# A one-core attention and feed-forward kernel: the 32x32 transposes of w3 read side-by-side columns and write to PSUM, the first block of w3 is turned by products with the identity, and the instructions stand in a new order

## The chip, the core and the metric

The kernel runs on one core of one Trainium2 chip. The metric is the device time of one execution in microseconds (us), lower is better. A profile is one execution, recorded instruction by instruction; its span reaches from the first to the last instruction of the program.

The engines are named as in the profile: PE is TensorE's matmul, PEld its weight load, DVE is VectorE, ACT is ScalarE, POOL is GpSimd, SP is SyncE, which here only issues DMAs. SBUF is the on-chip memory, PSUM the memory that TensorE writes its products to: eight banks, of 512 float32 columns each as the kernel uses them.

## What is computed

The reference is a Nystrom attention over 8 batches, 8 heads, 576 positions and 64 features per head, followed by a feed-forward part on the 4608 rows of width 512:

```python
def _attn_ref(q, k, v):
    q_lm = q.reshape(B, H, 32, S // 32, D).mean(axis=3)
    k_lm = k.reshape(B, H, 32, S // 32, D).mean(axis=3)
    A, Bm, C = sm(q, k_lm), sm(q_lm, k_lm), sm(q_lm, k)
    Z = Bm.transpose(0, 1, 3, 2) / (norm1(Bm) * norminf(Bm) + 1e-06)
    for _ in range(6):
        Z = 2 * Z - Z @ Bm @ Z
    return A @ Z @ C @ v

def _moe_ref(x, w1, w2, w3, w_out):
    a, b = x @ w1, x @ w2        # 512 -> 1024
    return (a * b @ w3) @ w_out  # 1024 -> 1024 -> 512
```

`sm` is a softmax of the scaled products. All inputs and the output are float32.

## The kernel before

**Two stages that overlap.** The kernel multiplies w3 by w_out once, into a float16 matrix `w34` of 1024 x 512, so that the dense part is `(a * b) @ w34`. Row block j (128 rows, j = 0 to 7) of `w34` needs row block j of w3, turned so that w3's columns lie on the partitions, and all of w_out. The first stage of the execution makes `w34`, block after block, and beside it the attention of the first batches. The dense part of batch 0 begins when all eight blocks and the first attention are done; from there on the dense part of one batch runs beside the attention of later ones, to the end.

**One block of w3.** For block j the steps are: `w3n{j}`, SP loads the 128 x 1024 float32 block (`load_w3`, line 323; for j = 0 in one DMA, for the others in four DMAs of 32 partitions, which put the quarter a of the columns on partitions 32a to 32a+31). `wt{j}{h}` turns it. For j = 0 TensorE does it with eight 128x128 transposes (`w3_ptr`, line 355) into three PSUM banks, in pieces of 1, 3 and 4. For j = 1 to 7 VectorE does it in two halves h (`w3_tr`, line 366): it transposes every 32x32 square, which together with the split over partitions by the DMA gives the turned block. The columns of one square are 8 apart in SBUF (`"p (b x c) -> p c b x"`, c = 8), and the result goes to the SBUF tiles `w3f`. `wh{j}{h}` on ACT (line 375) scales the result by 16 and rounds it to float16 (the high part), `wl{j}{h}` on DVE (line 382) makes the float16 remainder (the low part). TensorE then sums, over eight chunks c, high x high, high x low and low x high (`mh`, `mm`; 24 matmuls of 128 x 128 x 512 per block), and `wo{j}` on ACT (line 400) evicts the block. w_out is cut into high and low parts in the same way, chunk by chunk (`wf{c}` the load, `woh{c}` on ACT, `wol{c}` on DVE at line 341; for the chunks listed in `PWL` ACT scales at line 347 and POOL subtracts at line 352).

**One pair of heads-groups.** Task number n (0 to 15) is four heads of a batch. POOL issues the loads of k and q (`lq`, line 464, which also round to float16), SP those of v (`lv`, lines 475 and 478). DVE transposes in 32x32 squares (line 494, reading side-by-side columns); the mean over 18 positions is made by TensorE for n < 4 and by POOL after that (lines 502 and 509); then scores, softmax (DVE and ACT), and the normalisation `an` on POOL (line 654), which waits for DVE's reciprocal of line 648. POOL also issues the eight loads `lw` of w1 and w2 (line 484), which the first product of the dense part's up-projection (`U000`) needs, as it needs `wT` of the first group from DVE (line 893).

**What sets the order.** Each step is a task with an engine, an assumed duration, dependencies and a priority. A list scheduler in the kernel (`Plan.run`) places them with these assumed durations, and the instructions of each engine are then written out in the order found. On the chip each engine runs its own list in order and waits by semaphores; the assumed durations are no longer seen. So a change of an assumed duration or of a priority constant changes only the order. Rings of buffers (`P.ring`) are part of it: PSUM's six banks are the ring `P`.

Of the kernel before, what the change touches and what calls it, by code (L numbers as in the profile page):

```python
# [8 lines left out]
FP32 = mybir.dt.float32  # L9
# [6 lines left out]
S = 576  # L16
# [5 lines left out]
DM = 512  # L22
DF = 1024
HALF = 288
MP = 1.8
MT = 11.0
MY = 4.0
GR = int(2.0)
THIRD = 192
# [15 lines left out]
class Plan:  # L45
# [124 lines left out]
def kernel(  # L170
# [21 lines left out]
    def bank(i):  # L192
        return banks[i]
# [47 lines left out]
    def at(key, i=0):  # L241
        return P.slot[key][i]
# [19 lines left out]
    def att(n):  # L262
        bs = GROUPS[GOF[n // 2][0]]
        k = n - 2 * bs[0] - 2 * len(bs) + 4
        first = dense(bs[0]) - 51.0 + 8.0 * k
        return max(3.0 + 6.0 * n, first)

    def lane(g):
        return dense(GROUPS[g][0]) - 22.0

    def cvt(b):
        g, i = GOF[b]
        return lane(g) - 10.0 + 3.0 * (i + 2 - len(GROUPS[g]))

    NE = int(4.0)
    L0 = 4.0
    UO = 3.0
    GO = 8.0

# [19 lines left out]
    def const_e():  # L299
        nc.gpsimd.memset(vball[64:128, :, :, 4, :], 0.0)  # L300
        nc.gpsimd.memset(ecTall[64:128, :, 4, :], 0.0)
        nc.gpsimd.memset(lmTall, 0.0)

    def pads():
        for T in Tqs:
# [5 lines left out]
    add("cb", "POOL", 0.3, const_b, deps=["ca"], prio=-9)  # L311
    add("cc", "DVE", 0.8, const_c, deps=["cb"], prio=-5.0)
    add("cd", "ACT", 0.16, const_d, deps=["cb"], prio=-4.0)
    add("ce", "POOL", 2.8, const_e, prio=-4.0)


    def load_wout(c):
        def fn():
            nc.sync.dma_start(out=wof[at(f"wf{c}")],
                              in_=moe_w_out.rearrange("(p k) f -> k p f", k=8)[c])  # L320
        return fn

    def load_w3(j):
# [30 lines left out]

    def w3_ptr(j, h, c0, c1):
        def fn():
            ps, src = bank(at(f"ptr{j}{h}")), w3n[at(f"w3n{j}")].rearrange("p (x c) -> p c x", c=8)
            for c in range(c0, c1):
                nc.tensor.transpose(out=ps[:, 128 * (c - c0):128 * (c - c0) + 128], in_=src[:, c],
                                    identity=ident[:, :])  # L360
        return fn

    def w3_src(j, h, c0, c1):
        return bank(at(f"ptr{j}{h}"))[:, 0:128 * (c1 - c0)] if j < PEB else w3f[at(f"w3f{j}")][:, 128 * c0:128 * c1]

    def w3_tr(j, h):
        def fn():
            src = w3n[at(f"w3n{j}")].rearrange("p (b x c) -> p c b x", b=4, x=32)
            out_ = w3f[at(f"w3f{j}")].rearrange("p (c b y) -> p c b y", b=4, y=32)
            nc.vector.transpose(out=out_[:, 4 * h:4 * h + 4], in_=src[:, 4 * h:4 * h + 4])  # L370
        return fn

    def w3_hi(j, h, c0, c1):
# [5 lines left out]
    def w3_lo(j, h, c0, c1):  # L379
        def fn():  # L380
            c, t = slice(128 * c0, 128 * c1), w3t[at(f"w3t{j}")]
            nc.vector.scalar_tensor_tensor(out=t[:, 1, c], in0=w3_src(j, h, c0, c1), scalar=WSC,  # L382
                                           in1=t[:, 0, c], op0=ALU.mult, op1=ALU.subtract)
        return fn
# [16 lines left out]
                                 scale=1.0 / (WSC * WSC))  # L401
        return fn

    W1 = 1.0
    JS = int(4.0)
    JH = 2.0
    PWL = [(), (3,), (1, 4), (1, 3, 5), (1, 3, 5, 7)][int(3.0)]
    PEB = int(1.0)
    FIRST = [(0, 1), (1, 4), (4, 8)] if PEB else [(0, 4), (4, 8)]

    def w34_tasks():
        for j in range(8):
# [17 lines left out]
            for h, (c0, c1) in enumerate(cuts):  # L430
                k = (c1 - c0) / 4
                deps = [f"w3n{j}"] + ([f"wt{j}{h - 1}"] if h else [])
                if j < PEB:
                    add(f"wt{j}{h}", "PE", 0.44 * k, w3_ptr(j, h, c0, c1), deps=deps + ["cb"],
                        acq=[("P", f"ptr{j}{h}", 1, 2)], rel=[f"w3n{j}"], prio=p0 - 4.0 + h, mode="full")
                    src = f"ptr{j}{h}"
                else:
                    add(f"wt{j}{h}", "DVE", 0.62, w3_tr(j, h), deps=deps,
                        acq=[] if h else [("w3f", f"w3f{j}", 1, 4)], rel=[f"w3n{j}"], prio=p0 - 4.0 + 0.1 * h)
                    src = f"w3f{j}"  # L440
                add(f"wh{j}{h}", "ACT", 0.13 + 0.35 * k, w3_hi(j, h, c0, c1), deps=[f"wt{j}{h}"] + ([f"wh{j}0"] if h else []),
                    acq=[] if h else [("w3t", f"w3t{j}", 1, 8)], rel=[src], prio=p0 - 3.5 + h)
                add(f"wl{j}{h}", "DVE", 0.1 + 0.5 * k, w3_lo(j, h, c0, c1), deps=[f"wh{j}{h}"], rel=[src],
                    prio=p0 - 3.5 + h)
            part = {c: h for h, (c0, c1) in enumerate(cuts) for c in range(c0, c1)}
            for c in range(8):
# [233 lines left out]
    def quad_tasks(n):  # L680
# [16 lines left out]
        else:  # L697
# [4 lines left out]
                rel=[f"ls{n}"], prio=p - 5.0)  # L702
        add(f"lt{n}", "DVE", 0.24, lm_trans(n), deps=[f"tk{n}", f"mc{n}"], acq=[("lmu", f"lmu{n}", 1, 1)],
            rel=[f"lm{n}"], prio=p - 2.0)
        add(f"lc{n}", "ACT", 0.8, lm_place(n), deps=[f"lt{n}", "ce"], acq=[("lmT", f"lmT{n}", 1, 3)],
            rel=[f"lmu{n}"], prio=p - 1.5)
        both = [f"lc{n}"]
        add(f"S{n}", "PE", 0.52, s_mm(n), deps=both + [f"tk{n}"],
# [9 lines left out]
        add(f"sm{n}", "DVE", 0.8, s_max(n), deps=[f"S{n}"], acq=[("tiny", f"mx{n}", 1, 1)], prio=p)  # L718
# [377 lines left out]
    P.ring("w3n", 4)  # L1096
    P.ring("wf", 8)
    P.ring("w3t", 2)
    P.ring("w3f", 2)
    for i in range(NCH):  # L1100
        P.ring(f"ab{i}", 1)
    w34_tasks()
    for s in range(2):
        for qd in range(2):
            for wi in range(2):
                add(f"lw{s}{qd}{wi}", "POOL", 0.62, load_w12(s, qd, wi), prio=T0 - 13.0 + qd, after=T0 - 13.0 - 4.0,
                    move=1.46, lat=2.0)
    for n in range(NQ):
        quad_tasks(n)
# [10 lines left out]
    with tc.manual_schedule():  # L1120
        with tc.tile_pool(name="w34pool", bufs=1) as wp:
            w3n = [obig[:, 2 * i:2 * i + 2, :].rearrange("p a x -> p (a x)") for i in range(2)]
            w3n += [wp.tile([128, DF], FP32, name=f"w3n{i}") for i in (2, 3)]
            wof = [ecTs[i][:, 0:4, :].rearrange("p c x -> p (c x)") for i in range(4)]
            wof += [uu[i // 2][:, i % 2, :].bitcast(FP32) for i in range(4)]
            w3t = uu[2:4]
            wo = wp.tile([128, 2, 8, DM], FP16, name="wo")
            w3f = [wp.tile([128, DF], FP32, name=f"w3f{i}") for i in range(2)]
# [36 lines left out]
```

## Time and profile before

| | |
|---|---|
| time, median of 3 runs | 280.5 us (279.28, 280.71, 280.5) |
| the profiled execution: its time | 281.79 us |
| the profiled execution: its span | 280.0 us, granted TensorE clock 0.998 |
| busy share of the span | PE 93%, DVE 69%, ACT 70%, POOL 41% |
| DMA | 37.32 MB, 133 GB/s in the mean |
| the chain of waits, by engine | PE 67%, DMA 15%, ACT 5%, DVE 4% |

The shares are means over a first stage (to about 81 us), in which TensorE has gaps, and a second one in which it has almost none. DMA is in use by 0.8 to 1.1 of its 16 engines' time in the first 80 us and far less after that. The order within the first stage: block 0 of w3 is turned from 4.4 us, the last one (j = 7) from 71.23 us; the eight evictions `wo{j}` stand at 21.5 to 91.9 us; the first up-projection starts at 84.17 us.

### The profile page before, as it was taken

To read this page: it belongs to the slowest core of one execution; us is meant where nothing else is said; L and a number is where in the kernel's file an instruction comes from. 1 tells how busy PE (TensorE), PEld (TensorE's weight loads), DVE (VectorE), ACT (ScalarE), POOL (GpSimd) and SP (SyncE) were. 2 spreads that over 40 slices of the span, in tenths; PEclk is the share of its full clock that TensorE was granted. 3 is DMA by queue.
4 is the path that set the end of the run, shared out by engine and by line. 5 is a ranking of instruction groups with operands and counts; after the bars stand their busy time and mean duration, and the time that the engine had idled before them with its cause. 6 is when DMAs were issued, how large, how long until landed. Compare 5 with 4: busy or idle time off the path is not lost.

```text
span 280.0 us, 9565 instructions
## 1 busy us (share of the span) xinstructions
PE 260.4 (93%) x3824; PEld 169.5 (61%) x3824; DVE 192.3 (69%) x512; ACT 195.1 (70%) x551; POOL 113.8 (41%) x135
## 2 busy tenths in 40 slices
PE   3897679998899999999999999999999999999993
PEld 2244345553554885767677767667875674775762
DVE  3976799999978679776877777757666462442430
ACT  4645544963759988957888896589768656759551
POOL 9540381999499958899736011003001000000000
PEclk9999999999999999999999999999999999999999
DMA  7999899999964743999645431211121102121123
GB/s 226 304 231 251 228 193 241 220 195 217 230 118 86 116 93 49 256 239 208 126 125 159 135 117 40 69 46 41 56 63 40 42 37 77 57 96 40 75 77 114
DMA packets 30620, 37.32 MB, mean 133 GB/s; under 512 B 7792, under 2 KB 19824, under 8 KB 30576
## 3 DMA queue, kind: packets, MB, share of 16 engines
q1 hardware_dynamic: 24576, 24.92, 30.6%
q0 software_dynamic: 5760, 11.54, 23.8%
q8 instruction: 30, 0.49, 0.7%
q10 hardware_dynamic: 240, 0.26, 0.3%
q14 instruction: 14, 0.11, 0.1%
HBM read 38.80 MB, written 9.44 MB: 172 GB/s over the span
## 4 chain that ended last, share of the span: by engine, by line
PE 67%; DMA 15%; ACT 5%; DVE 4%; SPq 3%; issue 2%; POOL 2%; ACTq 0%
PE bank L247 61%; DMA vb<-in_v_dram 6%; DMA w3n<-in_moe_w_dram 5%; PE wide L247 4%; DMA w<-in_moe_w_dram 3%; PE wide L580 2%; DMA ecT<-in_moe_w_out_dram 2%; ACT lmT L539 2%; SPq L475 1%; ACT ec L572 1%; PE bank L663 1%; POOL ls L502 1%; POOL w L484 1%; DVE u L382 1%; SPq L331 1%
## 5 line engine op out<-in xcount | busy, mean ns | idle before, releaser
L247 PEld LDWEIGHTS <-u 128*128 128x128 f16 x960 | 80.3, 98 | 35.6 <-issue 7.4
L1000 DVE TENSOR_TENSOR ab<-asb,bank 128x192 f16<-128x192 f16 x192 | 60.6, 348 | 44.0 <-ACT asb L994 43.7
L247 PE MATMUL bank<-aT,u 128*128 128x192 f16 x768 | 78.6, 246 | 0.2
L247 PE MATMUL bank<-w,ab 128*128 128x512 f16 (+1 forms) x296 | 73.2, 373 | 0.0
L994 ACT CAST asb<-bank 128x192 f16<-128x192 f32 x192 | 56.4, 332 | 23.2 <-PE bank L247 20.4
L247 PE MATMUL bank<-wo,u 128*128 128x512 f16 x192 | 50.7, 394 | 2.0 <-ACT u L375 1.0
L654 POOL TENSOR_TENSOR ah<-ea,tiny 128x512 f16<-128x512 f32 (+1 forms) x16 | 18.7, 1173 | 76.5 <-DVE tiny L648 35.8
L247 PEld LDWEIGHTS <-ab 128*128 128x128 f16 x296 | 27.3, 98 | 20.7 <-issue 2.7
L509 POOL TENSOR_TENSOR ls<-ls 128x128 f32<-128x128 f32 (+2 forms) x48 | 36.1, 752 | 3.5
L911 ACT CAST u<-bank 128x512 f16<-128x512 f32 x64 | 34.3, 602 | 3.5 <-PE bank L247 3.2
L502 POOL TENSOR_TENSOR ls<-nat 128x1152 f32<-128x1152 f16 x12 | 29.0, 2413 | 13.1 <-ACT lm L516 13.0
L1026 ACT ACTIVATE osb<-bank 128x512 f32<-128x512 f32 x35 | 21.1, 603 | 11.6 <-PE bank L247 11.5
L539 ACT COPY lmT<-lmu 32x128 f16<-32x128 f16 x64 | 18.8, 294 | 4.2 <-DVE lmu L530 3.5
L247 PE MATMUL bank<-w,wT 64*32 64x512 f16 x512 | 18.5, 380 | 0.0
L247 PE MATMUL bank<-xz 32*32 32x64 f32 (+1 forms) x768 | 14.8, 213 | 1.4 <-DVE xz L857 1.4
L247 PEld LDWEIGHTS bank<-xz 32*32 32x32 f32 x768 | 11.1, 105 | 7.1 <-DVE xz L857 2.6
L572 ACT ACTIVATE ec<-wide,tiny 128x576 f32<-128x576 f32 x16 | 12.0, 750 | 4.7 <-DVE bsc L566 4.4
L641 ACT ACTIVATE ea<-ea 128x512 f32<-128x512 f32 (+1 forms) x16 | 11.0, 687 | 5.2 <-DVE ea L632 5.0
L375 ACT ACTIVATE u<-w3f 128x512 f16<-128x512 f32 x14 | 8.7, 629 | 8.2 <-DVE w3f L370 8.1
L647 DVE TENSOR_REDUCE tiny<-ea 128x16 f32<-128x512 f32 (+1 forms) x16 | 11.7, 734 | 2.7 <-ACT ea L641 2.7
L247 PEld LDWEIGHTS <-Tq 128*128 128x128 f16 x160 | 10.3, 97 | 5.4 <-issue 3.4
L558 DVE TENSOR_REDUCE tiny<-wide 128x1 f32<-128x576 f32 x16 | 11.7, 732 | 2.2 <-PE wide L247 2.1
(97 smaller groups left out, 330.2 us busy)
## 6 DMA issues: line engine op xcount, KB each, us to landing
vb<-in_v_dram SPq DMA_DIRECT2D x64, 128.0 KB, 4.6
out_dram<-osb SPq DMA_DIRECT2D x37, 128.0 KB, 2.3
nat<-in_k_dram POOLq DMA_DIRECT2D x16, 288.0 KB, 5.4
nat<-in_q_dram POOLq DMA_DIRECT2D x16, 288.0 KB, 7.1
out_dram<-osb SPq DMA_DIRECT2D x16, 256.0 KB, 2.6
w3n<-in_moe_w_dram SPq DMA_DIRECT2D x16, 128.0 KB, 7.4
w<-in_moe_w_dram POOLq DMA_DIRECT2D x8, 256.0 KB, 11.1
osb<-in_moe_w_dram SPq DMA_DIRECT2D x12, 128.0 KB, 4.1
```

What stands on the lines that cost most here:

```text
L247: nc.tensor.matmul(out_, lhsT, rhs, start=start, stop=stop, **({} if pos is None else {"tile_position": pos}))
L502: nc.gpsimd.tensor_tensor(out=l, in0=nat[:, :, 0:9, :], in1=nat[:, :, 9:18, :], op=ALU.add)
L509: nc.gpsimd.tensor_tensor(out=l[:, :, x:x + m, :], in0=l[:, :, x:x + m, :], in1=l[:, :, y:y + m, :], op=ALU.add)
L539: nc.scalar.copy(out=lm[r, :, h, :], in_=u[r].rearrange("p t l e -> p t (l e)"))
L558: nc.vector.reduce_max(out=mx[:, 0:1], in_=s_cols(), axis=AX.X)
L572: nc.scalar.activation(out=ecs[at(f"ec{n}")], in_=s_cols(), func=AXF.Exp, scale=SCALE, bias=tinies[at(f"mx{n}")][:, 1:2], accum_out=tinies ...
L647: nc.vector.reduce_sum(out=t[:, 20:20 + g], in_=eas[at(f"ea{n}")][:, 0:g, :], axis=AX.X)
L654: nc.gpsimd.tensor_tensor(out=ahs[at(f"ah{n}")][:, 0:g, :], in0=eas[at(f"ea{n}")][:, 0:g, :], in1=tinies[at(f"ta{n}")][:, 0:g].unsqueeze(2 ...
L911: nc.scalar.copy(out=uu[at(f"u{b}{qd}")][:, wi, 512 * half:512 * half + 512], in_=bank(at(f"pU{b}{wi}{half}{qd}")))
L994: nc.scalar.copy(out=asb[at(f"as{b}{j}{th}")], in_=bank(at(f"pD{b}{j}{th}"))[:, 0:THIRD])
L1000: nc.vector.tensor_mul(ab[:, j, c0:c0 + THIRD], asb[at(f"as{b}{j}{th}")], bank(at(f"pD{b}{j}{th}"))[:, THIRD:2 * THIRD])
L1026: nc.scalar.activation(out=osb[at(f"os{t}")], in_=bank(at(f"pE{t}")), func=AXF.Copy, scale=2.0 ** -12)
```

## The change

- The split over partitions of w3's columns becomes a = quarter, then c = chunk, then x = one of 32 columns, so that a 32x32 square has its 32 columns side by side. The rows of w_out are loaded in the order that fits it (`load_wout`): chunk c now holds, for each quarter a, 32 rows that lie one after the other.
- `w3_tr` reads those columns and writes to a PSUM bank of the ring `P`, one bank per half, in place of the SBUF tiles `w3f`, which are gone. `wh` and `wl` read the bank.
- `w3_ptr`, for block 0, makes four matmuls of a 128x32 weight with the 128x128 float32 identity in place of each transpose, one for each quarter of the columns, 32 matmuls in all.
- The constants: of w_out's chunks only number 3 is subtracted on POOL (before 1, 3 and 5); ACT's scaling of the other two goes away and DVE makes their low parts. The order's constants MP, MT, W1, JS, JH, L0 and some priorities and assumed durations change. The identity (`cb`) is made before the memsets of `ce`, and the largest of those runs on float32 words, half as many.
- What this does to the lists: SP issues chunks 1 to 4 of w_out ahead of block 1 of w3. POOL issues the eight loads of w1 and w2 after, and no longer before, the four sums of line 509 for n = 6, and two normalisations `an` stand among them: three loads, `an3`, two loads, `an4`, three loads. On TensorE, after the last product of `w34`, the tile shape changes 91 times, before 89 times.

```diff
-MP = 1.8
-MT = 11.0
+MP = 2.4
+MT = 8.0
...
-        return max(3.0 + 6.0 * n, first)
+        return max(6.0 + 6.0 * n, first)
...
-        return lane(g) - 10.0 + 3.0 * (i + 2 - len(GROUPS[g]))
+        return lane(g) - 8.0 + 3.0 * (i + 2 - len(GROUPS[g]))
...
-    L0 = 4.0
+    L0 = 3.0
...
-        nc.gpsimd.memset(lmTall, 0.0)
+        nc.gpsimd.memset(lmTall.rearrange("p i a l e -> p (i a l e)").bitcast(FP32), 0.0)
...
-    add("ce", "POOL", 2.8, const_e, prio=-4.0)
+    add("ce", "POOL", 2.4, const_e, deps=["cb"], prio=-4.0)
...
-                              in_=moe_w_out.rearrange("(p k) f -> k p f", k=8)[c])
+                              in_=moe_w_out.rearrange("(a k x) f -> k a x f", a=4, x=32)[c])
...
-            ps, src = bank(at(f"ptr{j}{h}")), w3n[at(f"w3n{j}")].rearrange("p (x c) -> p c x", c=8)
+            ps, src = bank(at(f"ptr{j}{h}")), w3n[at(f"w3n{j}")]
             for c in range(c0, c1):
-                nc.tensor.transpose(out=ps[:, 128 * (c - c0):128 * (c - c0) + 128], in_=src[:, c],
-                                    identity=ident[:, :])
+                for a in range(4):
+                    mm(ps[32 * a:32 * a + 32, 128 * (c - c0):128 * (c - c0) + 128],
+                       src[:, 256 * a + 32 * c:256 * a + 32 * c + 32], ident[:, :], pos=(0, 32 * a))
...
-        return bank(at(f"ptr{j}{h}"))[:, 0:128 * (c1 - c0)] if j < PEB else w3f[at(f"w3f{j}")][:, 128 * c0:128 * c1]
+        return bank(at(f"ptr{j}{h}"))[:, 0:128 * (c1 - c0)]
...
-            src = w3n[at(f"w3n{j}")].rearrange("p (b x c) -> p c b x", b=4, x=32)
-            out_ = w3f[at(f"w3f{j}")].rearrange("p (c b y) -> p c b y", b=4, y=32)
-            nc.vector.transpose(out=out_[:, 4 * h:4 * h + 4], in_=src[:, 4 * h:4 * h + 4])
+            src = w3n[at(f"w3n{j}")].rearrange("p (b c x) -> p c b x", b=4, x=32)
+            nc.vector.transpose(out=bank(at(f"ptr{j}{h}")).rearrange("p (c b y) -> p c b y", b=4, y=32),
+                                in_=src[:, 4 * h:4 * h + 4])
...
-    W1 = 1.0
-    JS = int(4.0)
-    JH = 2.0
-    PWL = [(), (3,), (1, 4), (1, 3, 5), (1, 3, 5, 7)][int(3.0)]
+    W1 = 5.0
+    JS = int(3.0)
+    JH = 3.0
+    PWL = [(), (3,), (1, 4), (1, 3, 5), (1, 3, 5, 7)][int(1.0)]
...
-                    add(f"wt{j}{h}", "DVE", 0.62, w3_tr(j, h), deps=deps,
-                        acq=[] if h else [("w3f", f"w3f{j}", 1, 4)], rel=[f"w3n{j}"], prio=p0 - 4.0 + 0.1 * h)
+                pe = j < PEB
+                add(f"wt{j}{h}", "PE" if pe else "DVE", 0.86 * k + 0.03 if pe else 0.64,
+                    (w3_ptr if pe else lambda j, h, c0, c1: w3_tr(j, h))(j, h, c0, c1), deps=deps + ["cb"],
+                    acq=[("P", f"ptr{j}{h}", 1, 2)], rel=[f"w3n{j}"], prio=p0 - 4.0 + h, mode="128x32" if pe else None)
...
-        add(f"lc{n}", "ACT", 0.8, lm_place(n), deps=[f"lt{n}", "ce"], acq=[("lmT", f"lmT{n}", 1, 3)],
+        add(f"lc{n}", "ACT", 1.22, lm_place(n), deps=[f"lt{n}", "ce"], acq=[("lmT", f"lmT{n}", 1, 3)],
...
-                add(f"lw{s}{qd}{wi}", "POOL", 0.62, load_w12(s, qd, wi), prio=T0 - 13.0 + qd, after=T0 - 13.0 - 4.0,
+                add(f"lw{s}{qd}{wi}", "POOL", 0.62, load_w12(s, qd, wi), prio=T0 - 10.0 + qd, after=T0 - 10.0 - 4.0,
```

More of the change, by code (lines that the diff above doesn't have):

```diff
@@ L432, in w34_tasks @@
                 deps = [f"w3n{j}"] + ([f"wt{j}{h - 1}"] if h else [])
[L433 to L437, printed above, removed]
-                    add(f"wt{j}{h}", "DVE", 0.62, w3_tr(j, h), deps=deps,
-                        acq=[] if h else [("w3f", f"w3f{j}", 1, 4)], rel=[f"w3n{j}"], prio=p0 - 4.0 + 0.1 * h)
-                    src = f"w3f{j}"
+                pe = j < PEB
+                add(f"wt{j}{h}", "PE" if pe else "DVE", 0.86 * k + 0.03 if pe else 0.64,
+                    (w3_ptr if pe else lambda j, h, c0, c1: w3_tr(j, h))(j, h, c0, c1), deps=deps + ["cb"],
+                    acq=[("P", f"ptr{j}{h}", 1, 2)], rel=[f"w3n{j}"], prio=p0 - 4.0 + h, mode="128x32" if pe else None)
                 add(f"wh{j}{h}", "ACT", 0.13 + 0.35 * k, w3_hi(j, h, c0, c1), deps=[f"wt{j}{h}"] + ([f"wh{j}0"] if h else []),
-                    acq=[] if h else [("w3t", f"w3t{j}", 1, 8)], rel=[src], prio=p0 - 3.5 + h)
-                add(f"wl{j}{h}", "DVE", 0.1 + 0.5 * k, w3_lo(j, h, c0, c1), deps=[f"wh{j}{h}"], rel=[src],
+                    acq=[] if h else [("w3t", f"w3t{j}", 1, 8)], rel=[f"ptr{j}{h}"], prio=p0 - 3.5 + h)
+                add(f"wl{j}{h}", "DVE", 0.1 + 0.5 * k, w3_lo(j, h, c0, c1), deps=[f"wh{j}{h}"], rel=[f"ptr{j}{h}"],
                     prio=p0 - 3.5 + h)
@@ L717, in quad_tasks @@
             ready.append(f"R{b}")
-        add(f"sm{n}", "DVE", 0.8, s_max(n), deps=[f"S{n}"], acq=[("tiny", f"mx{n}", 1, 1)], prio=p)
+        add(f"sm{n}", "DVE", 0.83, s_max(n), deps=[f"S{n}"], acq=[("tiny", f"mx{n}", 1, 1)], prio=p)
         new = n == 2 * GROUPS[GOF[b][0]][0]
@@ L1098 @@
     P.ring("w3t", 2)
-    P.ring("w3f", 2)
     for i in range(NCH):
@@ L1127 @@
             wo = wp.tile([128, 2, 8, DM], FP16, name="wo")
-            w3f = [wp.tile([128, DF], FP32, name=f"w3f{i}") for i in range(2)]
             for t in order[:first["w34"] + 1]:
```

## The prediction

> **What bounds the kernel now.** I cut the span into stages first, by the view of busy time in windows (columns: stretch, length, then busy us and instructions of PE, PEld, DVE, ACT and POOL, the clock, the DMA share, GB/s).
>
> ```profile
> 10.00:31.00 21.00, 18.84 (x131) 9.74 (x130) 15.14 (x26) 11.42 (x28) 6.46 (x9) 1.00 1.10 247
> 31.00:43.00 12.00, 8.00 (x59) 4.38 (x57) 10.91 (x20) 5.88 (x14) 7.83 (x8) 1.00 0.89 210
> 43.00:81.00 38.00, 34.66 (x570) 19.66 (x568) 36.42 (x81) 23.98 (x65) 28.05 (x31) 1.00 1.03 215
> 81.00:274.00 193.00, 192.75 (x3047) 132.39 (x3048) 124.62 (x374) 147.26 (x434) 64.04 (x68) 1.00 0.37 93
> ```
>
> From 81 to 274 us TensorE is busy 192.75 of 193: this part only begins earlier or later, it doesn't get shorter unless its order does. From 31 to 81 TensorE lacks 12 - 8.00 + 38 - 34.66 = 7.3 us, and DVE is the fullest engine with 10.91 + 36.42 = 47.3 of 50 us. From 10 to 31 the DMA engines are full (1.10) and DVE is not (15.14 of 21).
>
> The chain of waits (start, length, what) agrees: transfers early and again at 64 us, and the end all TensorE.
>
> ```profile
> 8.57 12.83 DMA w3n<-in_moe_w_dram
> 21.41 10.49 DMA vb<-in_v_dram
> ...
> 63.72 9.67 DMA w<-in_moe_w_dram
> ...
> 214.94 58.87 PE bank L247 x752
> ```
>
> Between 43.36 and 61 us it runs through DVE, ACT and POOL steps. So I treat 31 to 81 us as the stage that the change can shorten, with DVE as its gate, and look at what DVE does there (groups of that window; count, then busy us and mean ns).
>
> ```profile
> L382 DVE SCALAR_TENSOR_TENSOR u<-w3f,u 128x512 f16<-128x512 f32 x10 | 9.4, 952 | 0.2 <-ACT u L375 0.2
> L370 DVE STREAM_TRANSPOSE w3f<-w3n 128x512 f32<-128x512 f32 x6 | 6.4, 1073 | 1.5 <-DMA vb<-in_v_dram 1.5
> ...
> L370 DVE STREAM_TRANSPOSE w3f<-osb 128x512 f32<-128x512 f32 x4 | 4.3, 1096 | 0.0
> ...
> L494 DVE STREAM_TRANSPOSE Tq<-nat 128x512 f32<-128x512 f32 x3 | 2.0, 679 | 0.0
> ```
>
> Twenty of its 47 us are w3's: ten transposes and ten low parts. A transpose of the same 512 columns that reads them side by side (line 494) takes 679 ns against 1073 to 1096.
>
> **The change, part by part.** *Transposes on DVE.* Two groups of the whole run bound the write to PSUM:
>
> ```profile
> L530 DVE STREAM_TRANSPOSE lmu<-lm 128x64 f32<-128x64 f32 x16 | 3.5, 219 | 1.3 <-ACT lm L516 1.3
> L802 DVE STREAM_TRANSPOSE bank<-bm 128x128 f32<-128x128 f32 x4 | 1.3, 327 | 0.1
> ```
>
> From 64 columns (219) to 512 (679) SBUF costs (679 - 219)/448 = 1.03 ns per column, so 128 columns would be 285; the PSUM one takes 327, 42 more. If that is a fixed part, the new transpose costs 0.72 us; per column it is 0.68 + 4 x 0.042 = 0.85. I take 0.72, the shape of the nearer rows being a fixed start plus a line. Ten times 1.08 - 0.72 saves 3.6 us (2.3 at 0.85, 4.0 at 0.68).
>
> *Low parts.* They now read a bank. The one such row with 512 columns took 652 ns (block 0), the ten in the stage 952 in the mean, but their median over the run is 680 and their maximum 1906. The long ones (35.29 us, 1.91; 66.50, 1.58) lie beside POOL's sums. If a bank as source ends that, ten save 3.0 us; if not, 10 x 0.028 = 0.3. I take 2.7, since the five long ones all lie under POOL's work. The Trainium skill, "SBUF — State Buffer", section "Who interferes with whom", has the rule: a VectorE instruction with two SBUF inputs contends with a GpSimd one that reads SBUF, with one SBUF input it does not. By it the term would be the whole 3.0; the median row alone would say 0.3.
>
> *Two more low parts of w_out on DVE* (685 to 1184 ns each, +1.4 to 2.4 us), two subtractions (1.2 us each) gone from POOL and two scalings (0.6) from ACT. All before 20 us, where DVE sits idle 2.35 us at 23.5 and 1.55 at 30.7 until a w3 block has landed: hidden, cost 0; +1.4 if block 2 lands earlier than now.
>
> *Block 0 on TensorE.* Eight transposes took 1.97 us in all. The nearest row of 32-column products is 80 entries for 40 products of 64 columns in 1.34 us, 4 of them side by side; 32 of twice the width give (1.34 - 0.2)/40 x 2 x 32 + 0.2 = 2.0. Without overlap, at 110 ns of weight load each, 3.5. I take 0 extra; +1.5 at the other end, hidden while TensorE waits for w_out's chunks (matmuls come at 0.34 us from 8.61 to 14.8 where 0.24 is usual later). The Trainium skill, "Perfetto Trace Analysis", section "Transposes", speaks against this edit: a transpose should be issued as one and not as a matmul. By that the 3.5 would be nearer; the trace's 1.34 row says it is even.
>
> *Queues.* The identity is made on POOL before 3.3 us of memsets, but the first transposes, at 4.40, come 0.1 after block 0's landing (issued 0.74, landing in 3.5): gain 0.1, taken as 0. The loads of q and k start 0.7 us earlier. Block 1's four DMAs go behind four chunks of w_out: at 0.47 us per issue 1.9 us later, with the transfers ahead of them more; behind its transposes (7.35 now) DVE holds the first k transposes (14.11). Blocks 2 and 3 come after the same bytes as before, so the wait at 30.7 us stays: 0 on the path. That is the place where nothing is won: all w3 work before 31 us waits for DMA.
>
> *w1 and w2.* Now their eight issues (61.4 to 65.6 us, up to 14.1 to landing, so 79.7) are 4.4 us ahead of the first up-projection:
>
> ```profile
> 61.98 4.25 POOL L484 DMA_DIRECT2D w<-in_moe_w_dram  x7
> ...
> 84.17 0.62 PE L247 MATMUL bank<-w,wT 64*32 64x512 f16 x16
> ```
>
> In the new list 3.5 us of sums (line 509) go ahead of all eight, and two normalisations (1.3 and 1.05 us) ahead of the last five. POOL itself is earlier by what the front has won by 60 us, about half of 6.3; but landing is the pace of the full DMA engines (1.03) more than of the issue. So the landing stays near 79.7, and the first up-projection can come forward by about 4.4 us and no more. The last three chunks of block 7 follow it on TensorE's list, so the whole can win a little more.
>
> *The second part.* Two more changes of tile shape; around one, the weight loads show 0.42 us of idle: +0.8 at most, 0 at least (TensorE's own row is full); +0.4.
>
> **Sum.** DVE's relief is 3.6 + 2.7 = 6.3; the cover of w1 and w2 allows 4.4; I take the middle, 5.4, and add 0.4: -5.0. The profiled execution goes from 280.0 of span to 275.0 (281.79 to 276.8 of time); it was 1.3 above the median, so the median goes from 280.5 to **275.5 us**.
>
> **Rivals.** (a) *The relief is used whole*: w1 and w2 land earlier, because the loads of v beside them have gone ahead, and the stage loses all of TensorE's 7.3 us of gaps: 280.5 - 7.3 = 273.2, and 272.0 with the 0.7 us at the start and both extra low parts hidden. For: DMA shares over 1 are made of v loads too. Against: the 4.4 above. (b) *No cheaper transpose, or a stage paced by transfers.* If a PSUM write costs in proportion, 4 x 327 = 1.31 us, ten lose 2.3, low parts win 2.7, +0.4: 280.5. The same if the landings hold every step until 73 us, where the chain leaves w1 and w2: two low parts and no more are won. For: the chain of waits is DMA to 43 us. Against: 219 ns for 64 columns shows the large fixed part, and DVE is 95% full in the stage. (c) *Slower: w1 and w2 become the wait.* Mechanism: five of the eight issues stand behind `an3` and `an4`, and POOL's normalisations wait for DVE:
>
> ```profile
> POOL ah L654 <- DVE tiny L648: 35.8, 4, 16.5
> ```
>
> `an3` starts at 70.14 now. If it stays there, `an4` at 71.4 puts the last three issues at 72.4 to 74.3, and with the median of 11.1 us to landing they land at 85.4: the first up-projection at 85.5, 1.3 later than now, with 0.4 to 0.8 more for shapes: 282.5. It decides as soon as `an4` starts after about 69 us. Against: au3, on which it waits, is DVE work behind eight of the ten transposes and seven low parts, so it should come 4 to 5 us forward.
>
> **Chances.** The forecast 0.60, (a) 0.12, (b) 0.18, (c) 0.10. Range: low end (a), 272.0; high end, the poor ends of the terms together (2.3 + 0.3 won, 1.4 and 0.8 lost, so 279.8) with most of (b)'s partial forms: 272.0 to 279.8. About 0.5% (1.4 us) is what a measurement of this kernel can tell from none: below 279.1 is faster. Faster is the forecast, (a) and half of (b): 0.81; same is the other half and a bit of (c): 0.10; slower 0.09.
>
> **What would show it.** In the new profile: lines 370 and 382 (renumbered by a few) at about 0.72 and 0.65 us; the stage between 31 us and TensorE's full stretch 5 us shorter, with DVE's busy time there lower by 6; the landing wait near 30 us as it was; the first up-projection at 79 to 80 us, close behind the last landing of w1 or w2; the second part 193 us long. I am wrong if the transposes take over 1 us, if `an4` stands ahead of a late load of w1 or w2, or if TensorE has new gaps before 31 us that block 1's later loads made.

## The result and the profile after

The changed kernel takes 296.01 us (median of 4 runs, 294.98 to 297.22; the profiled execution 297.22, its span 295.1) against 280.61 for the kernel before on the same chip: a ratio of 1.0561, 95% interval 1.0508 to 1.0613. It is 15.4 us slower.

The view of busy time in windows of the kernel after (columns as in the prediction) shows where:

```profile
0.00:10.00 10.00, 4.02 (x65) 3.32 (x65) 1.74 (x10) 2.49 (x4) 6.33 (x20) 1.00 0.62 148
10.00:20.00 10.00, 1.46 (x3) 0.44 (x4) 1.45 (x3) 1.01 (x2) 0.00 (x0) 0.58 0.62 149
20.00:30.00 10.00, 5.59 (x13) 1.59 (x13) 4.96 (x8) 4.08 (x7) 3.27 (x5) 0.50 0.49 133
30.00:44.00 14.00, 9.17 (x57) 4.78 (x56) 5.64 (x12) 3.90 (x10) 1.06 (x2) 0.87 0.86 185
44.00:94.00 50.00, 49.66 (x652) 29.93 (x651) 43.84 (x105) 32.81 (x89) 34.17 (x38) 0.95 0.96 215
94.00:289.00 195.00, 193.94 (x3084) 133.07 (x3083) 126.68 (x380) 149.79 (x436) 64.13 (x69) 1.00 0.38 97
```

From 10 to 30 us TensorE is busy 7.05 of 20 us. Before, it was busy 18.84 of 21 there. Two more columns changed: the DMA share is 0.62 and 0.49 where it was 1.10, so the transfers are late although the DMA engines are *less* busy, and the granted clock is 0.58 and 0.50 where it was 1.00 (the last section says how far that column can be trusted). In the stage that the prediction was about, the wish came true: from 44 to 94 us TensorE lacks only 0.34 us (7.3 in the 50 us of before), and VectorE is no longer full (43.84).

The waits up to 50 us (who waited for whom: us in total, times, longest) name the late transfer:

```profile
DVE wo L341 <- ACT wo L336: 23.3, 7, 5.5
POOL wo L352 <- ACT ecT L347: 19.7, 1, 19.7
ACT wo L336 <- DMA ecT<-in_moe_w_out_dram: 14.8, 4, 5.6
PE bank L247 <- ACT wo L336: 13.7, 6, 4.8
ACT wo L336 <- DMA u<-in_moe_w_out_dram: 11.4, 4, 6.2
```

ScalarE's instructions that make the high parts of `w_out` (line 336) wait for the load of every one of the eight chunks, 26.2 us in all; VectorE, GpSimd and TensorE wait behind ScalarE. The kernel before has 0.9 us of this wait. The chain of waits starts the same way: the loads of `w_out` are its first 40 us.

```profile
3.15 19.67 DMA ecT<-in_moe_w_out_dram
...
22.84 19.84 DMA u<-in_moe_w_out_dram
...
42.71 0.64 ACT wo L336
```

SyncE is held as well. Its issues of the last four chunks (ns min/median/max), before and after:

```profile
L319 SPq DMA_DIRECT2D u<-in_moe_w_out_dram x4: 327/328/328, 5.1 to 6.7; - x4
```

```profile
L319 SPq DMA_DIRECT2D u<-in_moe_w_out_dram x4: 668/1455/5603, 4.0 to 22.8; - x4
```

SyncE issues in order, so the loads that stand behind these are issued late too: block 1 of `w3` from 9.64 us on and block 2 from 25.43 (3.56 and 9.79 in `one16`, experiment 9, which has the same order).

The bytes are the same; the number of packets is not. The DMA queue line of the page, before and after (the column behind the name counts packets):

```profile
q1 hardware_dynamic: 24576, 24.92, 30.6%
```

```profile
q1 hardware_dynamic: 24480, 24.92, 28.6%
```

96 packets are gone, 12 for each of the eight `w_out` loads, with no byte less (24.92 MB). A load that ends in one packet on each DMA engine that carried it would lose 12 when it runs on 4 engines instead of 16. That became theory E. Two runs of the next section bear the count out. `split_load` and `pair_load` load the same rows by 32 and 16 DMAs of 32 partitions instead of 8, and each additional DMA brings 16 packets (24 x 16 = 384 and 8 x 16 = 128 over 24576):

```profile
q1 hardware_dynamic: 24960, 24.92, 30.3%
```

```profile
q1 hardware_dynamic: 24704, 24.92, 31.3%
```

The new pattern, `"(a k x) f -> k a x f"` with `a=4`, has a leading dimension of 4; the old one, `"(p k) f -> k p f"`, leads with 128 partitions. The Trainium skill, "DMA: Bandwidth & Descriptors", section "Why a DMA increments its semaphore by 16 and not by 1", states such a rule: a DMA runs on the largest number of engines, at most 16, that divides the slowest dimension of both its patterns. By it these loads run on 4, and the 96 packets agree.

The last four chunks came in 19.84 us, 4 x 262144 B / 19.84 us = 53 GB/s. Before, 16 full engines moved 247 GB/s, so by this estimate 4 would move 62, less what other loads take of them: the size fits.

The instructions that the prediction priced (durations min/median/max) came out as forecast:

```profile
L370 DVE STREAM_TRANSPOSE bank<-w3n x8: 675/701/726, 46.2 to 87.8; 128x512 f32<-128x512 f32 x8
...
L383 DVE SCALAR_TENSOR_TENSOR u<-bank,u x17: 290/672/691, 5.4 to 90.5; 128x512 f16<-128x512 f32 x15, 128x128 f16<-128x128 f32 x1, 128x384 f16<-128x384 f32 x1
```

### The profile page after: what moved, and what is told of

Read it like the earlier page. It is cut to its first block, busy times and chain, and to the rows that moved or that the text cites. A ratio compares the mean times of both kernels' runs of the same rounds, so it can differ in the third digit from the quotient of the medians.

```text
span 295.1 us, 9681 instructions
## 1 busy us (share of the span) xinstructions
PE 265.6 (90%) x3880; PEld 174.1 (59%) x3880; DVE 184.3 (62%) x514; ACT 195.4 (66%) x549; POOL 109.0 (37%) x133
## 3 DMA queue, kind: packets, MB, share of 16 engines
q1 hardware_dynamic: 24480, 24.92, 28.6%
## 4 chain that ended last, share of the span: by engine, by line
PE 75%; DMA 13%; DVE 7%; issue 1%; ACT 1%; SPq 1%; DVEq 0%
PE bank L247 67%; DMA u<-in_moe_w_out_dram 7%; DMA ecT<-in_moe_w_out_dram 7%; PE wide L247 4%; PE wide L577 2%; PE bank L660 1%; DVE tiny L555 1%; DVE bank L370 1%; DVE u L383 1%; SPq L319 1%; ACT ec L569 1%; DVE ea L629 0%; DVE Tk L491 0%; PE wide L579 0%; DVE tiny L623 0%
## 5 line engine op out<-in xcount | busy, mean ns | idle before, releaser
L247 PEld LDWEIGHTS <-u 128*128 128x128 f16 x960 | 81.7, 99 | 54.4 <-issue 23.5
L997 DVE TENSOR_TENSOR ab<-asb,bank 128x192 f16<-128x192 f16 x192 | 59.9, 347 | 40.7 <-ACT asb L991 40.2
L247 PE MATMUL bank<-aT,u 128*128 128x192 f16 x768 | 76.9, 246 | 1.0 <-issue 0.9
L247 PE MATMUL bank<-wo,u 128*128 128x512 f16 x192 | 54.1, 413 | 19.6 <-ACT wo L336 13.7
L247 PEld LDWEIGHTS <-ab 128*128 128x128 f16 x296 | 26.7, 98 | 23.7 <-issue 5.7
L506 POOL TENSOR_TENSOR ls<-ls 128x128 f32<-128x128 f32 (+2 forms) x48 | 35.0, 728 | 3.7
L536 ACT COPY lmT<-lmu 32x128 f16<-32x128 f16 x64 | 18.8, 294 | 2.1 <-DVE lmu L527 1.5
L247 PE MATMUL bank<-xz 32*32 32x64 f32 (+1 forms) x768 | 14.8, 213 | 0.1
L376 ACT ACTIVATE u<-bank 128x512 f16<-128x512 f32 (+2 forms) x17 | 9.7, 572 | 5.8 <-DVE bank L370 3.3
L383 DVE SCALAR_TENSOR_TENSOR u<-bank,u 128x512 f16<-128x512 f32 (+2 forms) x17 | 10.8, 641 | 3.2 <-ACT u L376 3.1
```

The source lines that it names most:

```text
L247: nc.tensor.matmul(out_, lhsT, rhs, start=start, stop=stop, **({} if pos is None else {"tile_position": pos}))
L506: nc.gpsimd.tensor_tensor(out=l[:, :, x:x + m, :], in0=l[:, :, x:x + m, :], in1=l[:, :, y:y + m, :], op=ALU.add)
L536: nc.scalar.copy(out=lm[r, :, h, :], in_=u[r].rearrange("p t l e -> p t (l e)"))
L997: nc.vector.tensor_mul(ab[:, j, c0:c0 + THIRD], asb[at(f"as{b}{j}{th}")], bank(at(f"pD{b}{j}{th}"))[:, THIRD:2 * THIRD])
```

## The experiments

All ratios are to the kernel before, timed beside it; the interval is 95%. Times are medians.

**1. Each `w_out` load as four DMAs of 32 rows** (`split_load`), on the changed kernel:

```
-            nc.sync.dma_start(out=wof[at(f"wf{c}")],
-                              in_=moe_w_out.rearrange("(a k x) f -> k a x f", a=4, x=32)[c])
+            for a in range(4):
+                nc.sync.dma_start(out=wof[at(f"wf{c}")][32 * a:32 * a + 32],
+                                  in_=moe_w_out[256 * a + 32 * c:256 * a + 32 * c + 32, :])
```

> The changed kernel with each chunk of w_out loaded by four DMAs of 32 rows and 32 partitions in place of one DMA whose pattern begins with a dimension of 4. Same rows, same order, same arithmetic. Theory E (few engines): the one DMA is carried by 4 of the 16 DMA engines, 16 would carry it as before. Expects chunk 7 in use by about 22 us (34.8 in the changed kernel), w3's blocks 2 and 3 by about 32, and 274 to 281 us. Theory O (order): the four chunks ahead of block 1 and the other new priorities starve the front; expects 290 us or more. Theory R (rows): reading 32 neighbouring rows is slow on any number of engines; expects 290 or more.

Measured 284.15 us, ratio 1.0113 (1.0057 to 1.0169). Nearly 12 of the 15.4 us come back with the same data, layout and order. That is far from the 290 of theories O and R, and above the 281 that theory E allowed; what is left is in part the 32 issues on SyncE in the place of 8, as experiment 2, with half of them, takes 3.0 us less.

**2. The loads in pairs of chunks** (`pair_load`): half as many issues, two chunks in each DMA.

```
+            if c % 2:
+                return
...
+            for a in range(4):
+                nc.sync.dma_start(out=both[32 * a:32 * a + 32],
+                                  in_=moe_w_out[256 * a + 32 * c:256 * a + 32 * c + 64, :].rearrange("(i x) f -> x i f", i=2))
```

> The changed kernel with w_out loaded two chunks at a time, by four DMAs of 32 partitions for each pair, so 16 issues in place of 8 (and of 32 in the split kernel). Theory E: like the split kernel but up to 2 us better, since SP issues 7 us less: 273 to 280 us. Theories O and R: 290 or more.

Measured 281.12 us, ratio 0.9995 (0.9963 to 1.0027): 14.9 us back, and level with the kernel before, but not under it. Its windows:

```profile
10.00:20.00 10.00, 4.07 (x12) 1.09 (x12) 4.19 (x7) 3.68 (x8) 3.26 (x5) 0.70 1.11 251
20.00:31.00 11.00, 11.00 (x73) 6.46 (x72) 6.95 (x15) 3.52 (x10) 1.07 (x2) 0.81 1.11 243
31.00:43.00 12.00, 11.80 (x99) 7.34 (x97) 11.08 (x28) 9.50 (x26) 6.56 (x7) 1.00 0.84 202
43.00:79.00 36.00, 35.60 (x581) 21.12 (x580) 33.18 (x81) 24.16 (x66) 29.44 (x36) 1.00 1.06 222
79.00:272.00 193.00, 191.50 (x3036) 131.40 (x3034) 125.14 (x375) 147.54 (x432) 62.48 (x65) 1.00 0.38 97
```

The DMA engines are full again. From 31 to 79 us TensorE is busy 47.40 of 48 us (41.01 in the same window of before), so the stage gives 6.4 us. But TensorE has only 4.07 us of work from 10 to 20 us, at a clock of 0.70, and from 79 us on it lacks 1.5 us (0.25 before, from 81 us on). The gain is real and is lost at the start and, less, at the end. The chain at the start is the pairs and then `w3`'s block 1 (tile `osb`), whose four issues stand behind three pairs:

```profile
4.48 4.88 DMA ecT<-in_moe_w_out_dram
...
9.38 8.32 DMA osb<-in_moe_w_dram
```

**3. Only the new load pattern, on the kernel before** (`before_four`):

```
-                              in_=moe_w_out.rearrange("(p k) f -> k p f", k=8)[c])
+                              in_=moe_w_out.rearrange("(a k x) f -> k a x f", a=4, x=32)[c])
```

> The kernel before, in its own order, with only the pattern of the w_out loads changed to the one of the changed kernel. (Its product pairs rows of w_out with other columns of w3, so it computes another matrix; the work is the same.) Theory E: chunks land 4 to 7 us apart, 290 to 298 us. Theory R the same. Theory O: 279 to 282, as before.

Measured 303.18 us, ratio 1.0781 (1.0712 to 1.0851). Its waits up to 50 us show the same two rows as the changed kernel:

```profile
ACT wo L336 <- DMA ecT<-in_moe_w_out_dram: 15.0, 4, 6.1
ACT wo L336 <- DMA u<-in_moe_w_out_dram: 11.1, 4, 6.1
```

The pattern alone, with no other part of the change, costs 22 us, more than theory E's 298 allowed, and the same 96 packets are missing (24480).

**4. The changed kernel with the old columns and the old loads** (`old_columns`): the order, the transposes into PSUM and the products with the identity stay; a transpose, and a product of block 0, reads columns 8 apart again.

```
+                              in_=moe_w_out.rearrange("(p k) f -> k p f", k=8)[c])
...
-                       src[:, 256 * a + 32 * c:256 * a + 32 * c + 32], ident[:, :], pos=(0, 32 * a))
+                       src[:, 256 * a:256 * a + 256].rearrange("p (x c) -> p c x", c=8)[:, c], ident[:, :], pos=(0, 32 * a))
...
-            src = w3n[at(f"w3n{j}")].rearrange("p (b c x) -> p c b x", b=4, x=32)
+            src = w3n[at(f"w3n{j}")].rearrange("p (b x c) -> p c b x", b=4, x=32)
```

> The changed kernel with the columns of w3 and the rows of w_out as before (columns of a square 8 apart, a w_out chunk one DMA over 128 partitions), still in the new order, into PSUM, with products for block 0. Theory E: loads as before; the transposes at 1.05 to 1.15 us again; 277 to 282 us. Theory O: 290 or more. Theory R: 277 to 282. If the price of a transpose is set by the write to PSUM and not by the columns, the transposes stay at 0.70.

Measured 282.12 us, ratio 1.0046 (1.0011 to 1.0081). The transposes:

```profile
L370 DVE STREAM_TRANSPOSE bank<-w3n x8: 1070/1123/1131, 27.8 to 71.6; 128x512 f32<-128x512 f32 x8
```

Into PSUM, but over columns 8 apart, they take 1.12 us. So the write to PSUM saves nothing on a transpose; the side-by-side read does.

**5 and 6. Block 1 ahead of all `w_out` loads** (`pair_early`, `old_columns_early`): `W1 = 5.0` becomes `W1 = 1.0` in kernels 2 and 4.

> The pair kernel (changed kernel, w_out by pairs of chunks over all DMA engines) with the constant W1 back at 1.0: SP issues block 1 of w3 behind the first pair of chunks, no longer behind chunk 4. Theory S (start): what the pair kernel still lacks is lost between 11 and 19 us, where TensorE has no block 1 and its clock falls to 0.57 to 0.80 and the matmuls take twice as long. Expects block 1's transposes at 7 to 9 us in place of 17.7, clock 0.9 or more throughout, and 274 to 278 us. Theory D (DVE's relief is worth nothing): the stage of 31 to 81 us is set by transfers or by TensorE anyway; expects 279.5 to 282 us.

> The old_columns kernel (new order, columns 8 apart, one w_out DMA of 128 partitions per chunk) with W1 back at 1.0. It differs from pair_early by the columns and the w_out loads alone. Theory S with the relief real: 277 to 281 us, 2 to 4 us above pair_early. Theory D: the same as pair_early within 1 us.

Measured 283.13 us, ratio 1.0069 (1.0036 to 1.0102), and 283.39, 1.0101 (1.0059 to 1.0142): both worse than with block 1 late, so theory S fails. The two lie within 1 us of each other: in this order the shorter transposes show no worth (theory D). That block 1 comes late is not by itself what costs the start. The edit also changes the list that the planner makes, and in `pair_early` TensorE gets a new gap later (6.34 of 10 us busy from 60 to 70 us), so the two effects aren't separated.

**7. The kernel before with side-by-side columns** (`before_columns`): its own order, transposes into SBUF as before, the pair-wise loads, the products for block 0.

```
-            src = w3n[at(f"w3n{j}")].rearrange("p (b x c) -> p c b x", b=4, x=32)
+            src = w3n[at(f"w3n{j}")].rearrange("p (b c x) -> p c b x", b=4, x=32)
...
-                nc.tensor.transpose(out=ps[:, 128 * (c - c0):128 * (c - c0) + 128], in_=src[:, c],
-                                    identity=ident[:, :])
+                for a in range(4):
+                    mm(ps[32 * a:32 * a + 32, 128 * (c - c0):128 * (c - c0) + 128],
+                       src[:, 256 * a + 32 * c:256 * a + 32 * c + 32], ident[:, :], pos=(0, 32 * a))
```

> The kernel before, in exactly its own order, with only the columns changed: squares with side-by-side columns, still into the SBUF tiles, products with the identity for block 0, and w_out by pairs of chunks over all engines. If the columns alone are worth what the forecast's term said (transposes from 1.08 to 0.7, ten of them in the gated stage): 276 to 278.5 us, with the low parts as slow as before where POOL sums. Theory D: 279.5 to 282 us.

Measured 282.02 us, ratio 1.0036 (1.0004 to 1.0069), at theory D's end: the columns alone win nothing here, though the products for block 0 and twice the issues of `w_out` may hide a small gain. Two lines read together with kernel 4:

```profile
L376 DVE STREAM_TRANSPOSE w3f<-w3n x8: 653/670/705, 27.1 to 72.3; 128x512 f32<-128x512 f32 x8
...
L388 DVE SCALAR_TENSOR_TENSOR u<-w3f,u x14: 630/682/2474, 10.5 to 76.3; 128x512 f16<-128x512 f32 x14
```

Into SBUF with side-by-side columns the transpose is as short as into PSUM (670 against 701). But the low part that reads SBUF still has its long cases, up to 2474 ns, where the one that reads a bank in the changed kernel never passes 691. So each half of the change shortens one instruction: the columns the transpose, the bank the low part.

**8. Spare products while TensorE waits** (`pair_warm`): kernel 2 with 106 products of the identity with itself, whose result nobody reads, placed on TensorE's list between 11 and 19 us.

```
+            for _ in range({(0, 4, 0): 44, (0, 3, 1): 20, (1, 0, 0): 42}.get((j, c, part), 0)):
+                mm(psS[:, 0, 0:128], ident16[:, :], ident16[:, :])
```

> The pair kernel with 106 spare 128x128x128 matmuls of the identity into an unused PSUM tile, put on TensorE where it waits between 11 and 19 us. They change no result. Theory S splits into wait and clock: the wait stays, the clock should stay near 1.0. If the clock costs time, block 1's matmuls from 19 us on take 0.22 to 0.24 us and not 0.43, and the time is 2 to 4 us under the pair kernel: 277 to 279 us. If only the wait counts: the pair kernel's 281 within 1 us.

Measured 279.22 us (278.68 to 280.26, 12 runs), ratio 0.995 (0.9925 to 0.9976). The clock over 40 slices of the span, in `pair_load` and here:

```profile
PEclk9957999999999999999999999999999999999999
```

```profile
PEclk9999999999999999999999999999999999999998
```

The dip is gone with only these products added, and with it 1.3 us by the two ratios (1.9 by the medians, which were not measured side by side). The seven matmuls that follow block 1's landing take 1.69 us here and 3.17 in `pair_load`, and the first maximum of scores begins 1.3 us earlier, at 27.5 us. It is the fastest version of this study, 0.5% under the kernel before.

**9. The changed kernel with 16-engine loads** (`one16`): the load line of kernel 4 alone.

> The changed kernel with one thing undone: each w_out chunk is again loaded by one DMA whose pattern runs over 128 partitions, so that its rows no longer fit the columns of w3 (another matrix is computed, by the same instructions on the same bytes). Theory E (the leading dimension of 4 keeps a DMA on few engines, and that is the whole loss): all of the 15 us comes back and the chunks land as before; 278 to 281, under the pair-wise loads (281.1), which issue twice as many DMAs, or equal to them. Against the kernel with old columns (282.1), which differs from this one only in the columns that a transpose reads (1.10 us each there), it shows what the columns alone are worth: 1 to 4 us if the relief of VectorE counts, under 1 us if it does not (theory D). Rival (the new order or the products lose it as well): 285 or more.

Measured 280.48 us (278.88 to 283.42, 12 runs), ratio 0.9986 (0.9954 to 1.0018). One line is undone and 15.5 us come back: theory E. With its loads as before, the rest of the change is worth nothing that can be told from zero. Against `old_columns`, which differs in the columns that the transposes and block 0's products read, the two ratios differ by 0.6% with about 0.5% of uncertainty, so the shorter transposes are worth some 1.7 us of the whole, little of what they take off VectorE.

**10. Block 0 by VectorE too** (`pair_vector0`): `PEB = 0` in kernel 2, so no products with the identity.

> The pair-wise loads, and w3's block 0 loaded by four DMAs and transposed by VectorE in two halves like the other blocks, so that the 32 products with the identity fall away. Theory P (the products cost 1.3 to 1.7 us at the start): 279.5 to 280.5 against 281.1. Theory B (the start waits for bytes, and block 0 and block 1 cost the transfers the same whatever engine turns them): 281 to 282. Rival: block 0 in four DMAs of 1 KB rows lands later than in one of 4 KB rows and TensorE has nothing to do for longer: 283 or more.

Measured 285.48 us, ratio 1.0171 (1.0123 to 1.0219). Worse, as the rival of that expectation had it: TensorE's first 10 us hold 1.27 us of work instead of 4.42, and its chain shows a `w_out` load at 29% of the first 40 us. The edit moves block 0's issues as well as its transposes, so the price of the products can't be read from it.

**11. Block 1 after two pairs, with the spare products** (`pair_warm_early`): `W1 = 3.0` in kernel 8.

> The pair-wise loads with the spare products on TensorE (279.2), and w3's block 1 issued after two pairs of w_out rather than after three. If the wait for block 1 (8.3 to 10 us on the chain of waits up to 19 us) is what is left to win: block 1 lands about 2 us earlier, 277.5 to 278.5. If the bytes ahead of it only change places (w_out's last pairs land later by as much): 279 to 280. As with block 1 ahead of all w_out (283.1), where the list put score work later: 281 or more.

Measured 283.74 us, ratio 1.0075 (1.0033 to 1.0117). Block 1 lands earlier (17.5 against 18.9 us), but the list changes again and the first maximum of scores comes at 32.69 instead of 27.5 us. With experiments 5 and 6, three orders that bring block 1 forward all lose.

**12. Four of the loads issued by ScalarE's queue** (`pair_warm_two`):

```
-                nc.sync.dma_start(out=both[32 * a:32 * a + 32],
+                (nc.scalar if a % 2 and c < 4 else nc.sync).dma_start(out=both[32 * a:32 * a + 32],
```

> The kernel of the pair-wise loads with the spare products (279.2), where four of the sixteen w_out DMAs (two of each of the first two pairs) are issued by ScalarE's queue instead of SyncE's, so that SyncE reaches w3's block 1 some 1.7 us earlier (four issues of 0.43 us; block 1 issued at 5.4 instead of 7.1 us). If the issue of the DMAs on SyncE holds the start: 277.5 to 278.5. If the transfers hold it (235 to 247 GB/s from 5 us on, DMA share above 1), the landings stay where they are: 279 to 280. Rival: ScalarE issues behind its own work or w_out's last pair lands later: 281 or more.

Measured 279.7 us, ratio 0.9969 (0.9943 to 0.9994): no change from kernel 8. Its chain:

```profile
2.15 6.36 DMA ecT<-in_moe_w_out_dram
...
9.48 9.33 DMA osb<-in_moe_w_dram
```

Block 1 still lands at 18.8 us, as in kernel 8 (18.9). But it was not issued earlier, so the expectation's reasoning doesn't apply. SyncE's row for block 1 (start, length), in kernel 8 and here:

```profile
7.06 1.97 SPq L336 DMA_DIRECT2D osb<-in_moe_w_dram  x4
```

```profile
8.06 1.85 SPq L336 DMA_DIRECT2D osb<-in_moe_w_dram  x4
```

What SyncE waits for in this run's first 20 us says why:

```profile
SPq L324 <- DMA u<-in_moe_w_out_dram: 3.3, 4, 0.9
SPq L324 <- DMA ecT<-in_moe_w_out_dram: 3.2, 3, 2.3
```

It waits for earlier loads to land before it issues the next. In kernel 8's trace each of SyncE's issues from 5.9 us on begins 0.01 to 0.02 us after the landing of the load that SyncE issued eight places before (block 1 at 7.06, that landing at 7.04). So issues taken off SyncE gain nothing here: its list moves at the pace of the landings, with a DMA share of 1.08 from 10 to 20 us.

## Why the prediction was wrong, step by step

**The step that failed** is "Queues": "Blocks 2 and 3 come after the same bytes as before, so the wait at 30.7 us stays: 0 on the path", with block 1 only "1.9 us later, with the transfers ahead of them more". It counted bytes and issues and asked at what place in SyncE's list they stand, but not how many DMA engines would carry each load. The diff changes the DRAM pattern of the eight `w_out` loads to a leading dimension of 4, and the sum has no term for that. Shown in three ways: undone alone it gives back 15.5 us (`one16`), done alone it costs 22 (`before_four`), and the same rows in DMAs led by 32 partitions give back 14.9 (`pair_load`). The prediction's last condition, "if TensorE has new gaps before 31 us that block 1's later loads made", named the place of the loss but not the maker: it is `w_out`, not block 1. The price of 0.47 us per issue holds for SyncE's first issues alone: from there on its list moves at the pace of the landings (experiment 12), so loads on few engines also hold up every load behind them.

**Transposes: right.** Forecast 0.72 us, measured 0.70. The write to PSUM adds 0.03 us to a transpose (0.70 against 0.67 in experiment 7), where the forecast took 0.04 as a fixed part; the other bound, 0.85, is out.

**Low parts: right.** Forecast a median near 0.65 and no long cases; measured 0.672 and at most 0.691, against up to 2.5 in experiment 7 and 1.9 before:

```profile
L382 DVE SCALAR_TENSOR_TENSOR u<-w3f,u x14: 628/680/1906, 10.0 to 76.4; 128x512 f16<-128x512 f32 x14
```

The Trainium skill's rule in "SBUF — State Buffer", section "Who interferes with whom", agrees with these rows.

**Block 0's products: mis-sized.** Forecast 2.0 us against 1.97 for the transposes, 0 extra; the timeline of after (start, length, what, and in brackets the idle time before it) says 3.64, and `pair_load` has 3.27:

```profile
4.36 3.64 PE L247 MATMUL bank<-ident,osb 128*32 128x128 f32 x64 [4.36 <-DMA osb<-in_moe_w_dram]
```

The 64 entries are 32 products, so the nearest row (80 entries for 40 products, 4 side by side) had the right form but not the right price. The other end that the prediction named, 3.5 without overlap, is where it lies. The Trainium skill, "Perfetto Trace Analysis", section "Transposes", spoke for that end. The reason that the trace shows is the clock. In `pair_load` an entry takes 421 ns up to 6.9 us and 273 ns from 7.2 us on, when TensorE comes to its full clock (last section); the row that the forecast was worked from stands at 44.95 us, at full clock. Four entries side by side come every 0.21 us before the rise and every 0.11 after it, so at full clock the 64 would take about 2 us, an estimate from these rows: the forecast. The prediction read the same thing amiss in the matmuls that come at 0.34 us up to 14.8 us: it took them to be waiting for `w_out`, but up to 12 us they are themselves long, 620 ns and later 379. The 1.3 to 1.7 us stand at the start, where nothing hid them for certain; no run isolates what they cost the whole.

**The stage: more than forecast, but not all of it won.** The sum took 5.4 us from DVE's relief and cover; with full loads TensorE wins 6.4 us of its gaps between 31 and 79 us, nearly the 7.3 of rival (a). Part of that is work which the slower start had left over: over the whole run TensorE's idle time falls only from 19.6 us (280.0 of span less 260.4 busy) to 17.8 in `pair_load` (279.6 less 261.8), and its busy time grows by 1.4. The cover of `w1` and `w2` did not hold as the prediction had it. The first eviction of an up-projection comes forward from 85.6 to 82.3 us in `pair_load`, 81.2 in `pair_warm` and 80.1 in `one16`: 3.3, 4.4 and 5.5 us against "about 4.4 us and no more". The eight loads do not stay where they were either, but are issued later (65.0 to 71.6 us in `pair_load`, 61.4 to 65.6 before), and TensorE has no gap from 79 to 85 us in any of the three. So no run shows these loads as the limit that the sum took them for, and the whole still did not win 5.

**The start: taken at 0, lost nearly 4.** From 10 to 31 us TensorE was busy 18.84 us before. With loads over all engines it is busy 15.07 in `pair_load` and 15.29 in `one16`, whose rows are

```profile
10.00:20.00 10.00, 4.49 (x14) 1.45 (x13) 5.24 (x9) 2.77 (x5) 3.26 (x5) 0.70 1.09 251
20.00:31.00 11.00, 10.80 (x91) 6.90 (x90) 7.28 (x17) 5.38 (x14) 1.06 (x2) 0.96 1.10 249
```

So even without the four-engine loads the new front leaves TensorE 3.6 to 3.8 us more idle there, which eats most of the stage's 6.4. The first maximum of scores begins at 24.5 us before, 38.6 after, 28.8 in `pair_load` and 26.0 in `one16`. About 1.3 us of the loss is the clock (experiment 8). For the rest there are candidates (the products, block 1's place in the list) that no run separates; experiments 5, 6 and 11 show only that moving block 1 forward in the list is no remedy.

**The second part.** From the last eviction of the combined weight (line 400) to the end it took 188.1 us before, 189.8 after, 189.9 in `pair_load` and 188.5 in `pair_warm`. Forecast +0.4, at most +0.8; measured +0.4 to +1.8. `pair_load` and `pair_warm` have the same order but for the spare products at the start, so the 1.4 us between them are not the price of tile shapes; `pair_load` has one gap of 1.0 us here that `pair_warm` lacks, and the profile names no releaser for it.

**The rivals.** (c), a late `w1` or `w2`, did not decide, though its sign came: `an4` starts at 69.41 us in `pair_load`, past the 69 that it named. The first up-projection stands at 81.66 us there and not at 85.5, since the loads take at most 10.5 us to land (14.1 before), and where the stage runs undisturbed (44 to 94 us after, 43 to 79 in `pair_load`) TensorE has gaps of 0.3 and 0.4 us and no more. These small gaps also speak against (b)'s stage paced by transfers; its dear transpose is refuted by the 0.70 us. No rival had a load that becomes slower by itself. Two sums of the prediction are off, without weight for the outcome: the terms of (a)'s low end give 272.5, not 272.0, and those of the high end 280.1, not 279.8.

## What to carry to other kernels

A rearranged DRAM pattern is a change of price even if bytes, rows and row length stay: look at its leading dimension (4 against 128 or 32 here), and split the load so that many partitions lead. In the profile, a late load with a DMA share that *falls* (1.10 to 0.5 here) and packets that vanish without bytes (12 per load) is a load on few engines; with loads over all engines the share in the same stretch was 1.1. Where a queue's issues wait for earlier landings, as SyncE's do here, one slow load delays all that stand behind it. And when a layout is changed for one engine's sake, price every consumer of that layout, the loads among them, before pricing the engine.

## What the hardware showed beyond that

The granted TensorE clock fell to 0.50 from about 12 to 32 us in this kernel and from about 14 to 24 us in `pair_load`. Filling TensorE's gap with products that nobody reads kept it at 1.00 and won 1.3 to 1.9 us.

The column of the clock alone misleads at the start, though. These are the matmuls of 128x512 (count, then busy us and mean ns) from 14 to 30 us, in the changed kernel, where the column gives 0.50, and in `before_four`, where it gives 1.00:

```profile
L247 PE MATMUL bank<-wo,u 128*128 128x512 f16 x16 | 7.6, 619 | 13.0 <-ACT wo L336 7.2 <-ACT u L376 4.6 <-POOL wo L352 1.2
```

```profile
L247 PE MATMUL bank<-wo,u 128*128 128x512 f16 x17 | 8.0, 619 | 11.5 <-ACT wo L336 11.5
```

They are equally long. In the kernel before, with a column of 1.00 throughout, those from 6 to 12 us and those from 16 to 22 us are not:

```profile
L247 PE MATMUL bank<-wo,u 128*128 128x512 f16 x11 | 5.4, 620 | 1.0 <-ACT wo L336 1.0
```

```profile
L247 PE MATMUL bank<-wo,u 128*128 128x512 f16 x25 | 5.6, 379 | 0.0
```

So in these traces TensorE works at half clock from its first product on, and the column stays at 1.00 there until a first change is on record. By the durations, the full clock comes at about 12.5 us in the kernel before, 26 in `pair_vector0` and 30.5 in `before_four`; in the changed kernel and `pair_load`, whose products with the identity keep TensorE busy from 4.4 us on, between 7 and 8.5 us. In each of them 2.8 to 4.7 us of almost unbroken work stand before the rise (from 8.61 us on in the kernel before, from 27.22 in `before_four`). All eight kernels that have these products and no spare ones then fall back to 0.50 before 31 us; `before_four` does so at about 37 us, in a gap of 5.66 us. With the spare products in another order (`pair_warm_early`) the clock falls too, to 0.77 in the mean of 20 to 30 us. How long a gap brings the fall stays open.
